# A spectral filter followed by a softmax-weighted linear layer: the order of the opening's loads, and where the filter's sums run

## The chip, the cores and the metric

The kernel runs on one core of a Trainium2 chip. The metric is the time of one execution in microseconds (us), the median of several runs. A core has TensorE (PE, matrix products; PEld is its weight load), VectorE (DVE), ScalarE (ACT), GpSimd (POOL) and SyncE (SP). Each works through its own queue of instructions in order. SP, ACT and POOL also issue DMA transfers; all of these run on the same 16 DMA engines of the core.

## The reference

```python
X = np.fft.rfft(x, axis=1)                    # x: (8, 3136, 256), float32
y = np.fft.irfft(X * (filt_r + 1j * filt_i)[None], n=3136, axis=1)
t = y.reshape(8 * 3136, 256)
h = t @ w_in                                  # w_in: (256, 1024), given in float64
e = np.exp(h - h.max(-1, keepdims=True))
solu = h * (e / (e.sum(-1, keepdims=True) + 1e-9))
ln = (solu - solu.mean(-1, keepdims=True)) / np.sqrt(solu.var(-1, keepdims=True) + 1e-6) * g_ln
out = ln @ w_out                              # w_out: (1024, 256), given in float64
```

Eight images of 3136 tokens with 256 channels are filtered in frequency space along the tokens; then each token goes through a layer of width 1024.

## The kernel before, in words

The transform of length 3136 is split into 49 x 64. For each image there are four steps, each a matrix product with a fixed table: a first one over 49 rows (`first`), stored to a DRAM buffer d1; a second one over 64 (`forward`), whose result is multiplied by the filter (`multiply`); the second one back (`inverse`), stored to a DRAM buffer d2; and the first one back (`back`), which writes the tokens into the tile `y`. The layer then runs over `y` in blocks of 128 tokens (`product`, `exponential`, `normalize`, `project`); while it works on one image, the four steps of the next images are fitted between its blocks by a written plan.

The change touches the **opening**: the four steps of image 0, for which there is no layer work to lie beside, and the preparation of tables and weights. The order on each engine is as written in the source (a manual schedule; waits come from the data).

- *x.* `fetch_x` (line 527) reads image 0 in eight pieces of four columns (L530). A piece has two halves of 49 rows in the tile `rows_x`: h = 0 in order, h = 1 in reversed order. Before, SP issues h = 0 (48 rows of each piece, and the 49th row of all pieces as one 32 KB transfer) and POOL issues h = 1. Between POOL's pieces stand the loads of two raw weight blocks (`begin`, L420).
- *Stage one.* For each piece two matmuls (L233), one copy by ACT from PSUM over the piece itself (L235), and a store to d1 in two parts: 96 rows by ACT (L188), 4 rows by SP (L189). PSUM has three buffers for this.
- *Tables and filters.* `load_tables` (L476, L479) reads one table and eight blocks of filter rows for four or five row groups: (0, 4) and (4, 4) by POOL, (8, 5) by SP.
- *Idle matmuls.* `idle_row(5)` and later `idle_row(14)` (L558) are matmuls whose result nobody reads; one more stands in front of each `inverse`.
- *The spectrum loop* (lines 586 to 609) has seven units. For each: a fetch of d1 (L298), `forward` on PE (L308, tile pb), `multiply` (four multiplications on DVE, L329 and L330; and two sums, L331, the first of which runs on DVE and the second on POOL), `inverse` (L308, tile pc), copies by ACT (L346) and the store to d2 (L350). In PE's queue `forward` of unit i + 2 stands ahead of `inverse` of unit i. The products use two buffers each. `tables_back` (L492) turns the tables for the way back, by a matmul with the unit matrix `one`.
- *Weights.* The weights come as float64 words, in eight blocks; `convert` (lines 425 to 456) makes float32 of one: seven or eight operations on DVE, for blocks 0 to 3 one on ACT (L451) and two on POOL (L452, L456), for blocks 4 to 6 one on POOL. Conversions 0 and 1 stand ahead of the loop, the others behind it, with `weight_sums` (L152).
- *Behind the loop.* SP fetches d2 (L358) once the stores of d2 have landed, then six pieces of the second image's x (L471); PE runs `back` (L404, tile py) behind the idle row; then the layer's first product (L754) and its first operation on DVE (L778).

[...]

Of the kernel before, what the change touches and what calls it, by code (L numbers as in the profile page):

```python
# [9 lines left out]
FP32 = mybir.dt.float32  # L10
# [7 lines left out]
P = 128  # L18
# [76 lines left out]
def kernel(  # L95
# [95 lines left out]
    class Spectrum:  # L191
# [24 lines left out]
        def fetch_x(self, i, halves, out=None):  # L216
            if out is None:
                out = self.pools["r"].tile([P, NCH, C], FP32, name=f"x_{self.e}_{i}", tag="r")
            self.xs[i] = out
            xb = x[self.e]  # L220
            for h, first, step in ((0, NCH * i, C), (1, N2 - 1 - NCH * i, -C)):
                halves[h](out[N1 * h:N1 * h + N1],
                          bass.AP(tensor=xb.tensor, offset=xb.offset + first * C,
                                  ap=[[N2 * C, N1], [step, NCH], [1, C]]))
# [186 lines left out]
    with ExitStack() as st:  # L411
# [53 lines left out]
        def spare_piece(i):  # L465
            return spare[i % 2][:, i // 2 * NCH * C:(i // 2 + 1) * NCH * C].rearrange(
                "p (n c) -> p n c", c=C)
# [6 lines left out]
        def load_tables(i0, n, dma):  # L474
            de = fpool.tile([P, n, 2, 2, NQ], FP32, name=f"de_{i0}", tag=f"de{i0}")
            dma(out=de[:, :, 0].rearrange("p i u q -> p i (u q)"), in_=there_dram[:, i0:i0 + n, :])  # L476
            f = fpool.tile([P, n, 2, C], FP32, name=f"f_{i0}", tag=f"f{i0}")
            for place, k, held, rows in all_filter_rows(i0, n):
                dma(out=f[place, 0:held, k, :], in_=rows)  # L479
            for i in range(n):  # L480
                tables[i0 + i], filters[i0 + i] = (de, i), (f, i)
# [36 lines left out]
        def begin(j):  # L518
            raws[j] = load_words(weights[j][1], j)
# [13 lines left out]

        st.enter_context(tc.manual_schedule())
        nc.sync.dma_start(out=wf_t, in_=wf_dram)
        nc.scalar.dma_start(out=one, in_=one_dram)
        pieces = NH // NCH

        fetch_x(0, 0, NCH, 0, N1 - 1, nc.sync.dma_start)
        fetch_x(0, 0, NH, N1 - 1, 1, nc.sync.dma_start)  # L540
        for i in range(pieces):
            if i:
                fetch_x(0, NCH * i, NCH, 0, N1 - 1, nc.sync.dma_start)
            fetch_x(1, NCH * i, NCH, 0, N1, nc.gpsimd.dma_start)
            if i in (4, 7):
                begin(i // 7)
        load_tables(0, 4, nc.gpsimd.dma_start)
        load_tables(4, 4, nc.gpsimd.dma_start)
        for i in range(pieces):
            sp.xs[i] = rows_x[:, NCH * i:NCH * i + NCH]  # L550

# [4 lines left out]
        def idle(out):  # L556

            nc.tensor.matmul(out=out, lhsT=tables[0][0][:, 0, 0].rearrange("p u q -> p (u q)"),  # L558
                             rhs=filters[0][0][:, 0], start=True, stop=True)

        def idle_row(count, name):
            for j in range(count):
                idle(ps_h.tile([P, 2, C], FP32, name=f"{name}_{j}", tag="h"))

        idle_row(5, "idle")

        def convert(j):
            load_float64(weights[j][0], raws.pop(j), negate=j < 4, share=j < 4,
                         add=(nc.vector if j == 7 else nc.gpsimd).tensor_tensor)

        for j in range(2):
            convert(j)

        def start(i):
            sp.fetch_filter(i)
# [3 lines left out]
        units = len(sp.units)  # L579

        sp.fetch(0, nc.sync.dma_start)
        for i in range(1, units - 2):
            sp.fetch(i, nc.sync.dma_start, spare_piece(i - 1))
            if i == 3:
                load_tables(8, NP - 8, nc.sync.dma_start)
        for i in range(2):
            start(i)
            tables_back(4 * i, 4)
        for i in range(units):
            if i == 2:  # L590
                tables_back(8, NP - 8)
            if i + 2 < units:
                start(i + 2)
            sp.multiply(i, 0, nc.vector.tensor_tensor)
            sp.multiply(i, 1, nc.gpsimd.tensor_tensor)
            pss = [ps_t.tile([P, 2, C], FP32, name=f"pc_0_{i}_{u}", tag="t") for u in range(2)]
            idle(pss[0])
            sp.inverse(i, pss)
            sp.store(i, nc.scalar.dma_start)
            if i == 0:  # L600
                nc.gpsimd.dma_start(out=wi_t, in_=wi_dram)
                nc.gpsimd.dma_start(out=wq_t, in_=wq_dram)
                nc.gpsimd.dma_start(out=wb_t[:, 0:N1], in_=wb_dram)
                nc.gpsimd.dma_start(out=g_sb, in_=moe_g_ln.rearrange("(k p) -> p k", p=P))
            elif i == 1:
                for last_one in (units - 2, units - 1):
                    sp.fetch(last_one, nc.gpsimd.dma_start, spare_piece(last_one - 1))
            for j in {2: (2,), 3: (3, 4), 4: (5,), 5: (6,)}.get(i, ()):
                begin(j)
        idle_row(14, "idler")  # L610
        rows_t4 = pools["r"].tile([P, NH, C], FP32, name="t4_0", tag="r")
# [5 lines left out]
        for i0, n, rows in ((0, 4, P), (4, 4, P), (8, NP - 9, P), (NP - 1, 1, NQ)):  # L617
# [2 lines left out]
                out=f_dram[i0:i0 + n].rearrange("i u q k c -> (u q) i (k c)")[0:rows],  # L620
                in_=f[0:rows, at:at + n].rearrange("p i k c -> p i (k c)"))
        convert(2)
        convert(3)
        begin(7)
        convert(4)
        weight_sums(w_in_sb)
        for j in (5, 6, 7):
            convert(j)
        for ch in range(pieces):
# [537 lines left out]
```

## Time and profile before

| what | value |
|---|---|
| median of 3 runs | 1595.84 us (1594.65 to 1599.87) |
| span of the profiled execution | 1598.0 us |
| its span against the median | 2.2 us longer; no time around the span is listed |
| PE busy | 1548.0 us, 97% |
| DVE busy | 1310.2 us, 82% |
| POOL busy | 1177.0 us, 74% |
| ACT busy | 915.8 us, 57% |
| DMA | 311.14 MB, mean 195 GB/s |
| first matmul on x | at 11.76 us |
| first product of the layer on PE | at 97.05 us |

How to read it: the span runs from the first to the last recorded instruction. "Busy" of an engine is the time in which it works; a wait is not busy. In a timeline row stand the start, the length, the engine, the source line, the operation and the tiles (result <- operands), and in brackets how long the engine had been idle and what ended it; "x16" means that neighbouring rows of one kind are merged. "SPq" is an issue by SP's queue. In a row of the windows view stand the stretch, its length, the busy time of PE, PEld, DVE, ACT and POOL with the number of instructions, the granted TensorE clock as a share of full speed, the mean busy share of the 16 DMA engines, and the GB/s that they moved. The landing of a transfer is the time of its last completion signal in the trace.

### The profile page before, as it was taken

The page shows a single profiled execution, that of the slowest core. Times are in us where ns is not written, and L with a number is a line of the kernel's source. Part 1 is how long each engine was busy: PE and PEld are TensorE (multiplying, and loading weights), DVE is VectorE, ACT ScalarE, POOL GpSimd, SP SyncE. Part 2 cuts the span into 40 slices and gives each one's busy share as a digit, 9 for nine tenths or more (in the row PEclk, how much of TensorE's full clock was granted, in tenths as well). Part 3 has the DMA queues.
Part 4 walks back from the last instruction along what each step waited for, and adds up shares of the span by engine and source line. Part 5 has one row for each costly group of instructions (what it writes and reads, how often), then busy time and mean ns, then how long its engine had stood idle before and what let it go on. Part 6 is the DMA issues. An engine that isn't in the chain of part 4 may idle for free. (4 is left out here: it accounts for less than half of the span.)

```text
span 1598.0 us, 37061 instructions
## 1 busy us (share of the span) xinstructions
PE 1548.0 (97%) x12828; PEld 1055.5 (66%) x12828; DVE 1310.2 (82%) x2639; ACT 915.8 (57%) x1825; POOL 1177.0 (74%) x1371
## 2 busy tenths in 40 slices
PE   5998999999999999999999999999999999999997
PEld 1463567666666676667766776667776777777777
DVE  1887888998998889888988889987898777777773
ACT  2245655656565656565566656665555666665653
POOL 4555986688768867886778877886866867677775
PEclk8999999999999999999999999999999999999999
DMA  9989978776987588766886678766784544343434
GB/s 261 288 272 261 262 214 236 215 228 175 247 245 231 157 230 238 230 177 169 235 240 195 166 196 256 209 183 174 222 220 127 134 125 127 96 113 99 113 103 115
DMA packets 343804, 311.14 MB, mean 195 GB/s; under 512 B 27835, under 2 KB 310100, under 8 KB 343620
## 3 DMA queue, kind: packets, MB, share of 16 engines
q1 hardware_dynamic: 271476, 170.45, 40.4%
q0 software_dynamic: 33744, 98.81, 20.6%
q10 hardware_dynamic: 38400, 39.53, 8.2%
q8 instruction: 104, 1.70, 0.5%
q14 instruction: 80, 0.65, 0.1%
HBM read 124.51 MB, written 81.40 MB: 129 GB/s over the span
## 5 line engine op out<-in xcount | busy, mean ns | idle before, releaser
L885 PEld LDWEIGHTS o<-w_out_sb,solu_t 128*128 128x128 f32 x3136 | 381.5, 192 | 50.2 <-issue 43.2
L885 PE MATMUL o<-w_out_sb,solu_t 128*128 128x128 f32 x3136 | 401.5, 276 | 3.8 <-DVE ot L905 3.1
L754 PE MATMUL m<-w_in_sb,s 128*128 128x512 f32 x784 | 397.9, 608 | 2.1 <-ACT h L764 1.4
L885 PEld LDWEIGHTS o<-w_out_sb,u 128*128 128x128 f32 x2352 | 305.9, 191 | 140.7 <-issue 104.0
L802 DVE SCALAR_TENSOR_TENSOR h<-e,rsum,h 128x1024 f32<-128x1024 f32 x196 | 321.2, 1639 | 6.9
L885 PE MATMUL o<-w_out_sb,u 128*128 128x128 f32 x2352 | 310.4, 275 | 3.0 <-POOL u L733 2.1
L754 PE MATMUL m<-w_in_sb,y 128*128 128x512 f32 x588 | 306.6, 604 | 3.0 <-DVE h L775 2.1
L764 ACT COPY h<-m 128x512 f32<-128x512 f32 x294 | 173.2, 589 | 201.8 <-PE m L754 193.6
L901 ACT ACTIVATE ot<-o,rs_t 128x128 f32<-128x128 f32 x392 | 143.2, 366 | 248.0 <-PE o L885 244.6
L733 POOL TENSOR_TENSOR u<-solu_t 128x512 f32<-128x512 f32 x98 | 133.5, 1362 | 178.3 <-DMA solu_t<-turn 157.0
L810 ACT ACTIVATE h<-h,nmu 128x1024 f32<-128x1024 f32 x196 | 224.6, 1146 | 47.0 <-DVE turn L818 37.4
L818 DVE STREAM_TRANSPOSE turn<-h 128x1024 f32<-128x1024 f32 x196 | 243.1, 1241 | 3.1
L778 DVE CUSTOM_DVE_ANT_0 h<-m,h 128x512 f32<-128x512 f32 x196 | 133.2, 679 | 131.6 <-ACT h L764 94.5
L786 ACT ACTIVATE e<-h,nmax 128x1024 f32<-128x1024 f32 x196 | 225.1, 1148 | 20.1 <-DVE h L802 18.8
L733 POOL TENSOR_TENSOR u<-solu_t,u 128x512 f32<-128x512 f32 x98 | 147.6, 1506 | 94.0 <-PE o L885 94.0
L754 PEld LDWEIGHTS m<-w_in_sb,s 128*128 128x128 f32 x784 | 127.9, 190 | 88.0 <-issue 68.3
L905 DVE SCALAR_TENSOR_TENSOR ot<-o,rs_t,ot 128x128 f32<-128x128 f32 x299 | 103.7, 347 | 73.8 <-ACT ot L901 55.6
L733 POOL TENSOR_TENSOR u<-u,solu_t 128x512 f32<-128x512 f32 x98 | 152.0, 1551 | 15.2 <-PE o L885 7.2
L733 POOL TENSOR_TENSOR solu_t<-solu_t,solu_t 128x512 f32<-128x512 f32 x98 | 161.8, 1651 | 0.9
L754 PEld LDWEIGHTS m<-w_in_sb,y 128*128 128x128 f32 x588 | 96.3, 190 | 98.1 <-issue 54.7
L733 POOL TENSOR_TENSOR s<-y 128x128 f32<-128x128 f32 x196 | 97.9, 500 | 0.5
L381 PEld LDWEIGHTS py<-wb_t,t 50*64 50x64 f32 x3584 | 57.6, 134 | 42.9 <-issue 22.5
(126 smaller groups left out, 2001.6 us busy)
## 6 DMA issues: line engine op xcount, KB each, us to landing
solu_t<-turn SPq DMA_DIRECT2D x780, 128.0 KB
out_dram<-ot SPq DMA_DIRECT2D x196, 128.0 KB
t<-d POOLq DMA_DIRECT2D x112, 200.0 KB, 6.8
d<-x POOLq DMA_DIRECT2D x100, 200.0 KB, 5.0
f<-f_dram POOLq DMA_DIRECT2D x39, 512.0 KB, 8.2
t<-d ACTq DMA_DIRECT2D x37, 512.0 KB
d<-g POOLq DMA_DIRECT2D x36, 512.0 KB, 4.9
x<-in_x_dram SPq DMA_DIRECT2D x112, 98.0 KB
```

The costliest lines, as they stand in the source:

```text
L381: nc.tensor.matmul(out=views[g][64 * h:64 * h + 64, cb, i, :], lhsT=t4[rows, i, c0:c0 + 64], rhs=wb_t[rows, 0:N1], start=True, stop=True)
L733: nc.gpsimd.tensor_tensor(out=out, in0=in0, in1=in1, op=op)
L754: nc.tensor.matmul(out=ms[j, bank], lhsT=lhsT, rhs=w_in_sb[:, w, :], start=m in (1, 2, 7), stop=True, skip_group_check=True)
L764: nc.scalar.copy(out=h_half(k, i), in_=ms[j, 0])
L778: nc.vector.tensor_tensor_reduce(out=h_half(k, i), in0=ms[j, bank], in1=h_half(*kept), scale=1.0, scalar=sofar, op0=ALU.add, op1=ALU.min, ...
L786: nc.scalar.activation(out=e, in_=hs[k], func=AFT.Exp, bias=nmaxs.pop(k)[:, 1:2], scale=-1.0, accum_out=esum)
L802: nc.vector.scalar_tensor_tensor(out=solu, in0=e, scalar=rsum, in1=solu, op0=ALU.mult, op1=ALU.mult, accum_out=nmu)
L810: nc.scalar.activation(out=solu, in_=solu, func=AFT.Square, bias=nmu, scale=-float(DFF), accum_out=variances[g][:, i:i + 1])
L818: nc.vector.transpose(out=turns[g][:, :, i, :], in_=solus[k].rearrange("p (f j) -> p f j", j=32))
L885: nc.tensor.matmul(out=pos[p, bank], lhsT=lhs[:, f, :], rhs=w[:, f, :], start=f == 0 and (m in (1, 2, 7) or alone), stop=True, skip_group_ ...
L901: nc.scalar.activation(out=out_half(p, *to)[0], in_=pos[p, 0], func=AFT.Copy, scale=rs)
L905: nc.vector.scalar_tensor_tensor(out=ot, in0=pos[p, bank], scalar=rs, in1=out_half(p, *kept)[0], op0=ALU.mult, op1=ALU.add)
```

## The change

x goes first: both halves of a piece are issued in turn, h = 0 by SP and h = 1 by ACT, 48 rows each, and both 49th rows behind the first piece; `one` follows on ACT. POOL's first work is a copy of one column that waits until the fourth piece of x has landed (`once_landed`); then it issues the tables (0, 4). DVE fills a part of `y`, and two matmuls on it stand at the head of PE's queue. The idle row ahead of the loop has 6 matmuls instead of 5, and the idle matmul in front of each `inverse` has half the columns.

SP's order becomes: fetches of d1 for units 0 and 1, tables (4, 4), fetches 2 and 3, tables (8, 5), fetches 4 to 6, and four small constants that POOL fetched before. POOL waits until fetch 0 has landed, and then issues raw weight blocks 0 and 1; blocks 2 to 5 follow in the loop, behind units 1, 2, 4 and 5, block 6 behind conversion 2 and block 7 behind conversion 3. Conversions 0 and 1 move into the loop, behind units 2 and 4. Both sums of `multiply` run on POOL. `weight_sums` moves ahead of conversion 4.

```diff
@@ -533,19 +533,29 @@
 
         st.enter_context(tc.manual_schedule())
         nc.sync.dma_start(out=wf_t, in_=wf_dram)
+        pieces = NH // NCH
+
+        for i in range(pieces):
+            for h, dma in ((0, nc.sync.dma_start), (1, nc.scalar.dma_start)):
+                fetch_x(h, NCH * i, NCH, 0, N1 - 1, dma)
+                if i == 0:
+                    row, at = N1 * h + N1 - 1, N2 * (N1 - 1) + NH * h
+                    dma(out=rows_x[row:row + 1, ::-1 if h else 1, :], in_=x[0, at:at + NH, :].rearrange(
+                        "(o n) c -> o n c", o=1))
         nc.scalar.dma_start(out=one, in_=one_dram)
-        pieces = NH // NCH
-
-        fetch_x(0, 0, NCH, 0, N1 - 1, nc.sync.dma_start)
-        fetch_x(0, 0, NH, N1 - 1, 1, nc.sync.dma_start)
-        for i in range(pieces):
-            if i:
-                fetch_x(0, NCH * i, NCH, 0, N1 - 1, nc.sync.dma_start)
-            fetch_x(1, NCH * i, NCH, 0, N1, nc.gpsimd.dma_start)
-            if i in (4, 7):
-                begin(i // 7)
+
+        seen = small.tile([P, 1], FP32, name="seen", tag="seen")
+
+        def once_landed(ap):
+            nc.gpsimd.tensor_copy(out=seen[0:ap.shape[0]], in_=ap)
+
+        once_landed(rows_x[0:NR, NCH * 3, 0:1])
         load_tables(0, 4, nc.gpsimd.dma_start)
-        load_tables(4, 4, nc.gpsimd.dma_start)
+        warm = y[:, 0, 0:512]
+        nc.vector.memset(warm, 1.0)
+        for n in range(2):
+            nc.tensor.matmul(out=ps_t.tile([P, 512], FP32, name=f"warm_{n}", tag="t"), lhsT=warm[:, 0:P],
+                             rhs=warm, start=True, stop=True)
         for i in range(pieces):
             sp.xs[i] = rows_x[:, NCH * i:NCH * i + NCH]
 
@@ -556,20 +566,17 @@
         def idle(out):
 
             nc.tensor.matmul(out=out, lhsT=tables[0][0][:, 0, 0].rearrange("p u q -> p (u q)"),
-                             rhs=filters[0][0][:, 0], start=True, stop=True)
+                             rhs=filters[0][0][:, 0, 0:len(out.shape) - 1], start=True, stop=True)
 
         def idle_row(count, name):
             for j in range(count):
                 idle(ps_h.tile([P, 2, C], FP32, name=f"{name}_{j}", tag="h"))
 
-        idle_row(5, "idle")
+        idle_row(6, "idle")
 
         def convert(j):
             load_float64(weights[j][0], raws.pop(j), negate=j < 4, share=j < 4,
                          add=(nc.vector if j == 7 else nc.gpsimd).tensor_tensor)
-
-        for j in range(2):
-            convert(j)
 
         def start(i):
             sp.fetch_filter(i)
@@ -579,10 +586,19 @@
         units = len(sp.units)
 
         sp.fetch(0, nc.sync.dma_start)
-        for i in range(1, units - 2):
+        sp.fetch(1, nc.sync.dma_start, spare_piece(0))
+        once_landed(sp.t2s[0][:, 0, 0:1])
+        for j in range(2):
+            begin(j)
+        load_tables(4, 4, nc.sync.dma_start)
+        for i in range(2, 4):
             sp.fetch(i, nc.sync.dma_start, spare_piece(i - 1))
-            if i == 3:
-                load_tables(8, NP - 8, nc.sync.dma_start)
+        load_tables(8, NP - 8, nc.sync.dma_start)
+        for i in range(4, units):
+            sp.fetch(i, nc.sync.dma_start, spare_piece(i - 1))
+        for held, source in ((wi_t, wi_dram), (wq_t, wq_dram), (wb_t[:, 0:N1], wb_dram),
+                         (g_sb, moe_g_ln.rearrange("(k p) -> p k", p=P))):
+            nc.sync.dma_start(out=held, in_=source)
         for i in range(2):
             start(i)
             tables_back(4 * i, 4)
@@ -591,21 +607,15 @@
                 tables_back(8, NP - 8)
             if i + 2 < units:
                 start(i + 2)
-            sp.multiply(i, 0, nc.vector.tensor_tensor)
+            sp.multiply(i, 0, nc.gpsimd.tensor_tensor)
             sp.multiply(i, 1, nc.gpsimd.tensor_tensor)
             pss = [ps_t.tile([P, 2, C], FP32, name=f"pc_0_{i}_{u}", tag="t") for u in range(2)]
-            idle(pss[0])
+            idle(pss[0][:, 0, :])
             sp.inverse(i, pss)
             sp.store(i, nc.scalar.dma_start)
-            if i == 0:
-                nc.gpsimd.dma_start(out=wi_t, in_=wi_dram)
-                nc.gpsimd.dma_start(out=wq_t, in_=wq_dram)
-                nc.gpsimd.dma_start(out=wb_t[:, 0:N1], in_=wb_dram)
-                nc.gpsimd.dma_start(out=g_sb, in_=moe_g_ln.rearrange("(k p) -> p k", p=P))
-            elif i == 1:
-                for last_one in (units - 2, units - 1):
-                    sp.fetch(last_one, nc.gpsimd.dma_start, spare_piece(last_one - 1))
-            for j in {2: (2,), 3: (3, 4), 4: (5,), 5: (6,)}.get(i, ()):
+            if i in (2, 4):
+                convert(i // 2 - 1)
+            for j in {1: (2,), 2: (3,), 4: (4,), 5: (5,)}.get(i, ()):
                 begin(j)
         idle_row(14, "idler")
         rows_t4 = pools["r"].tile([P, NH, C], FP32, name="t4_0", tag="r")
@@ -620,10 +630,11 @@
                 out=f_dram[i0:i0 + n].rearrange("i u q k c -> (u q) i (k c)")[0:rows],
                 in_=f[0:rows, at:at + n].rearrange("p i k c -> p i (k c)"))
         convert(2)
+        begin(6)
         convert(3)
         begin(7)
+        weight_sums(w_in_sb)
         convert(4)
-        weight_sums(w_in_sb)
         for j in (5, 6, 7):
             convert(j)
         for ch in range(pieces):
```

## The prediction

> **What bounds the kernel now.** I read the windows view first, in stretches of ten microseconds, then the timeline of the first 105 us, then the landings of single transfers in the trace. The windows say where the kernel can still change.
>
> ```profile
> 0.00:10.00 10.00, 0.00 (x0) 0.00 (x0) 0.06 (x1) 0.00 (x0) 6.28 (x12) 1.00 0.83 171
> 10.00:20.00 10.00, 8.24 (x14) 3.04 (x15) 0.00 (x0) 3.58 (x4) 2.66 (x4) 1.00 1.05 220
> 20.00:30.00 10.00, 8.27 (x20) 2.96 (x18) 5.77 (x13) 5.80 (x6) 3.71 (x7) 1.00 1.02 388
> 30.00:40.00 10.00, 3.64 (x4) 1.00 (x4) 2.04 (x4) 1.23 (x2) 7.01 (x12) 0.53 0.85 268
> 50.00:60.00 10.00, 9.34 (x110) 5.68 (x103) 8.49 (x13) 3.42 (x8) 7.95 (x11) 1.00 1.01 291
> 200.00:1500.00 1300.00, 1288.83 (x11317) 898.06 (x11317) 1110.86 (x2245) 782.24 (x1573) 989.37 (x1152) 1.00 0.68 189
> ```
>
> The columns after the length are PE, PEld, DVE, ACT, POOL, granted clock, DMA share, GB/s. The last row is the rest of the kernel: PE is busy 1288.83 of 1300 us. Nothing there is edited, so what the opening saves or loses passes to the end. The opening is DMA's: its share is 0.83 to 1.05 from the start, at only 171 and 220 GB/s while x is read, and 388 once stores of d1 join the reads.
>
> ```profile
> 11.76 16.52 PE L233 MATMUL pa<-x,wf_t 98*100 98x512 f32 x32 [11.76 <-DMA x<-in_x_dram]
> 36.30 7.19 PE L558 MATMUL idle<-f,de 128*128 128x512 f32 x10 [8.02 <-DMA f<-in_filt_r_dram]
> 37.28 0.40 SPq L298 DMA_DIRECT2D t<-d  x1
> 44.63 0.69 DVE L329 TENSOR_TENSOR pr<-pb,f 128x512 f32<-128x512 f32 x1 [12.52 <-PE pb L308]
> 50.93 0.69 DVE L329 TENSOR_TENSOR pr<-pb,f 128x512 f32<-128x512 f32 x1
> 52.25 1.38 DVE L331 TENSOR_TENSOR pr<-pr,pt 128x512 f32<-128x512 f32 x1
> 68.09 0.41 DVE L432 TENSOR_SCALAR raw<-raw 128x512 int32<-128x512 int32 x1
> 68.32 0.77 POOL L331 TENSOR_TENSOR pi<-pi,pt 64x256 f32<-64x256 f32 x1 [0.33 <-DVE pt L330]
> 70.66 12.28 PE L558 MATMUL idler<-f,de 128*128 128x512 f32 x28
> 82.78 14.43 PE L404 MATMUL py<-wi_t,t 100*128 100x98 f32 x128
> 103.34 0.69 DVE L456 TENSOR_TENSOR w_out_sb<-w_out_sb,raw 128x512 f32<-128x512 f32 x1
> 103.95 0.68 DVE L778 CUSTOM_DVE_ANT_0 h<-m,h 128x512 f32<-128x512 f32 x1
> ```
>
> Read them as stations. Matmuls on x start at 11.76. The first fetch of d1 goes out at 37.28, because the last store of d1, issued at 29.73, lands at 37.26 behind table traffic. The filter's product starts at 44.63 (unit 2 at 50.93); DVE leaves it at 68.09, POOL's last sum ends at 69.09. From 68.09 DVE is busy without a gap with conversions 2 to 7, to 103.95, where it takes the first product. PE's own line is 70.66, 82.78, 97.05.
>
> **Stage one.** Removed from ahead of d1's last store: both raw loads (1.05 MB) and the second table set (1.28 MB). Added ahead of the stores: nine x transfers on ACT's queue. [...] x to there is five pieces, 1.97 MB: at 220 GB/s 9.0 us, from the first packet at 2.3, plus 1.2 from last packet to landing (the 32 KB row: packet ends 7.19, landed 8.40) and 0.8, half of that row's 1.69 us on its one DMA engine: 13.3. Issue 0.37, table load 1.28, copy 1.01: 16.0. Three PSUM buffers hold pieces 0 to 2, so PE starts piece 3 there; five pieces at 1.72 (the pitch of copies before, 19.73 to 21.44) end at 24.6, the copy at 25.7, the store is issued at 26.0. By bytes: 1.6 MB of x and tables left at 16 plus 3.07 of d1 at 400 GB/s end at 27.7, and 1.2 to land. **T, the first fetch, is 28.9** against 37.28 (bounds 27 and 31: ACT freed at 11.7 or 14.5, and the byte sum at 350 GB/s).
>
> The two warming matmuls cost nothing: PE has no work there. They may save part of 3.4 us (four pieces' halves at 0.86 instead of 0.43), but ACT's copy, not PE, releases piece 3, so I count zero. POOL's copy that waits for x's fourth piece holds back the first tables to about 12; they need 1.28 MB, some 8 us, and are wanted by the idle row at 24.6: covered by 4 us.
>
> [...]
>
> **From T to unit 2.** The fetch of 512 KB lands 4.1 after issue (37.28 to 41.48): 33.0. Eight forward matmuls 1.11; DVE starts unit 0 at 34.2, 10.4 earlier. Then SP's order bites. Before, fetches 0 to 3 were issued back to back; now the table set for units 2 and 3 (nine transfers, 1.31 MB) stands between fetch 1 and fetch 2. PE's queue holds pb_2 ahead of the first inverse, and DVE's unit 2 needs the buffer that this inverse frees. [...] In bytes: two fetches, tables, one fetch, 2.9 MB at 370 GB/s plus 1.1 and 1.2 of ends is T+10.1; with both raw loads, which POOL now issues when fetch 0 has landed, in between (1.05 MB, 2.8 us) T+13. I take T+12, as the raw loads start some 3 us after POOL issues them: **40.9**, against 44.79. PE has then stood idle 5 us, and the clock falls, as after 28.3 (0.53 in the row 30 to 40, matmuls of the idle row at 1.06 instead of 0.43). So pb_2 2.0, idle 0.9, half of the inverse 1.0: **unit 2 starts at 44.8**, against 50.93. Of 10.4 gained 6.1 are left.
>
> **The product.** Removed from DVE: one sum per unit, five of 0.69 to 0.74, one of 1.38, a small one of 1.00. Added to POOL at 1.28 each (0.77 the small one), 8.5 us. Moved into DVE's row, behind units 2 and 4: conversions 0 and 1, which lay in dead time at 21.84 and 27.91. Alone a conversion takes 3.96 (21.84 to 25.80); beside POOL's sums up to 7.0 (72.46 to 79.49, two operations of 0.43 taking 1.5, one of 0.69 taking 1.66). I take 4.9, nearer to the first, since POOL's two sums cover only its first 2.6 us. DVE: four multiplications a unit, 2.44. Unit 2 to 47.2, conversion 52.1, unit 3 54.5, unit 4 57.0 (fetch 4 lands by T+23 = 52, behind nine more table transfers; it binds only if over 3 us late), conversion 61.9, unit 5 64.3, unit 6 at 1.6: **65.9 against 68.09, 2.2 earlier**. POOL: the second conversion's two operations stand ahead of unit 5's sums: 63.2, a raw load's issue 0.8, two sums 2.6, a load 0.8, two small sums 1.5: **68.9 against 69.09**. The last inverse comes about 0.9 earlier, since its idle matmul is halved.
>
> **To the end.** PE's line: 14 idle matmuls as before, so py and the first product come 0.9 earlier; it had slack (1.24 us on x of the second image at 103.1). DVE's line keeps its 35.9 us: first product 2.2 earlier. DMA's line: fetches of d2 start when its last store lands (75.74); 2.2 earlier, as fewer raw loads are queued there, but raw 6, issued at 67.17 before, now falls among the fetches: 0.52 MB at 283 GB/s is 1.9, leaving 0.3. Between 0.3 and 2.2 I take 1.5. The constants fetched by SP instead of POOL, and the shorter idle matmuls (0.43 each, DVE or POOL sets the pace), count zero; without that cover they are 3 us for six. Sum: 1598.0 - 1.5 = 1596.5. The profiled span is 2.2 over the median 1595.84, so I forecast **1594.3**.
>
> **Rivals.** *Data come in time.* T at 27, fetch 2 at T+10.1 = 37.1, PE warm: pb_2 1.1, idle 0.4, 0.8: unit 2 at 39.4. Conversions at 4.0 make 19.3 instead of 21.1: DVE leaves at 58.7, POOL at 61.7, 7.4 earlier, less 0.4 for raw 6: 7.0, median 1588.8. For it: reads in 1 KB packets ran at 350 GB/s (40 to 44 us), and x's reversed half now comes so. Against: SP's in-order queue.
> *The conversions collide with the sums (slower).* Both take 7.0: DVE leaves at 70.1. POOL's share of a conversion waits for DVE and stands ahead of the next unit's sums, 4.2 and one unit's 2.6 more: last sum at 75.7, 6.6 late, py with it; less PE's 1.2 slack 5.4, median 1601.2. It decides when the stretch of both exceeds the 2.2 that DVE gains. For it: the rows at 72.46. Against: the first conversions need no POOL until near their end.
> *x is no earlier.* ACT, held by its own x transfers, starts copying at 18, T is 32: 3.1 later than forecast, 1.6 over now, median 1597.4. The change then only trades waits.
>
> **Chances.** Forecast 0.47, x no earlier 0.12, data in time 0.27, collision 0.14. About 0.3% (4.8 us) is what a measurement of this kernel can tell from no change: faster 0.27, same 0.59, slower 0.14. The range reaches nearly to both outer cases: 1588 to 1601.5.
>
> **What would show it.** Right: first copy of ACT near 15, first fetch of d1 near 29, DVE's unit 0 near 34, then a DVE wait of some 5 us on pb_2, with the clock at half; DVE's third conversion near 66. Wrong: no wait there (data in time), or conversions of over 6 us and POOL's last sum past 72 (collision), or a fetch of d1 after 31. If the stations move as forecast and the end does not, the line from d2's fetches to the second image was mis-sized.

## The result, and the profile after

| kernel | median | range | runs |
|---|---|---|---|
| before, beside it | 1597.86 us | 1594.65 to 1600.28 | 4 |
| changed | 1639.35 us | 1637.67 to 1640.49 | 4 |

The ratio is **1.0266** (95% interval 1.0246 to 1.0287): 42 us slower. The forecast was 1594.3 us, with a range up to 1601.5. The profiled execution of the changed kernel has a span of 1638.1 us. Lines up to the edit keep their numbers; behind it L558 is now L568, L733 L744, L754 L765.

The windows of the changed kernel (columns as before):

```profile
50.00:60.00 10.00, 9.27 (x77) 5.26 (x78) 4.91 (x8) 2.15 (x4) 2.67 (x2) 0.69 0.96 221
60.00:70.00 10.00, 6.10 (x56) 3.23 (x54) 5.58 (x10) 2.48 (x5) 0.04 (x1) 0.83 0.68 200
70.00:80.00 10.00, 4.85 (x29) 2.54 (x32) 5.43 (x8) 1.07 (x2) 7.98 (x7) 0.67 0.31 105
80.00:90.00 10.00, 4.06 (x27) 1.92 (x22) 5.43 (x12) 1.74 (x3) 6.00 (x6) 0.50 0.44 149
200.00:1500.00 1300.00, 1278.97 (x11265) 885.43 (x11264) 1109.08 (x2221) 770.71 (x1553) 993.23 (x1153) 1.00 0.74 192
```

Two things are to be seen. From 60 to 90 us nothing is full: in one of the three rows POOL works 0.04 us of ten, in another the DMA share falls to 0.31, and PE and DVE are half idle throughout; so there is a chain of waits. And in the long last row, where no line was edited, PE is busy 1278.97 us instead of 1288.83, with a DMA share of 0.74 instead of 0.68 for nearly the same GB/s (192 and 189).

Matched instruction by instruction with the kernel before, PE's work is 25.3 us late at its first product (122.33 against 97.05), 26.4 at 250 us, and some 40 at the end. So some 25 us are lost in the opening and 14 to 15 more, bit by bit, in the body, which is everything behind the first product. That product in the kernel before:

```profile
97.05 1.93 PE L754 MATMUL m<-w_in_sb,y 128*128 128x512 f32 x4
```

The stations of the changed kernel, in the timeline:

```profile
7.36 7.06 PE L233 MATMUL pa<-x,wf_t 98*100 98x512 f32 x12 [2.13 <-DMA x<-in_x_dram]
15.84 1.01 ACT L235 COPY x<-pa 100x1024 f32<-100x1024 f32 x1
25.16 1.01 ACT L235 COPY x<-pa 100x1024 f32<-100x1024 f32 x1 [2.53 <-DMA d<-x]
32.45 0.40 SPq L298 DMA_DIRECT2D t<-d  x1
38.49 0.69 DVE L329 TENSOR_TENSOR pr<-pb,f 128x512 f32<-128x512 f32 x1 [37.06 <-PE pb L308]
55.02 0.69 DVE L329 TENSOR_TENSOR pr<-pb,f 128x512 f32<-128x512 f32 x1 [10.06 <-PE pc L308]
91.35 0.89 POOL L331 TENSOR_TENSOR pi<-pi,pt 64x256 f32<-64x256 f32 x1
94.71 13.51 PE L568 MATMUL idler<-f,de 128*128 128x512 f32 x28
108.06 14.43 PE L404 MATMUL py<-wi_t,t 100*128 100x98 f32 x128
122.33 1.93 PE L765 MATMUL m<-w_in_sb,y 128*128 128x512 f32 x4
```

DVE's unit 0 is 6.1 us earlier than before (38.49 against 44.63), unit 2 is 4.1 later, POOL's last sum 23.0 later. What lies between the last two of these is the loop; its chain of waits, in the timeline:

```profile
57.42 0.59 DVE L432 TENSOR_SCALAR raw<-raw 128x512 int32<-128x512 int32 x1
63.35 2.01 PE L308 MATMUL pb<-y,de 64*64 64x256 f32 x16 [3.00 <-DMA y<-d]
66.44 0.45 PE L308 MATMUL pc<-pr,de 64*64 64x256 f32 x2
67.66 1.07 ACT L346 COPY g<-pc 128x512 f32<-128x512 f32 x2 [6.74 <-PE pc L308]
69.23 0.65 ACT L451 ACTIVATE raw<-raw 128x512 f32<-128x512 int32 x1 [0.50 <-ACT g L346]
69.96 1.29 POOL L452 TENSOR_TENSOR raw<-raw,power 128x512 f32<-128x512 f32 x1 [10.82 <-ACT raw L451]
73.16 1.27 POOL L331 TENSOR_TENSOR pr<-pr,pt 128x512 f32<-128x512 f32 x1
74.48 1.13 PE L308 MATMUL pc<-pr,de 64*64 64x256 f32 x4 [5.38 <-POOL pr L331]
83.90 1.29 POOL L452 TENSOR_TENSOR raw<-raw,power 128x512 f32<-128x512 f32 x1 [5.82 <-ACT raw L451]
```

Read it from POOL's 10.82 backwards. POOL stands at its part of conversion 0 (L452), which needs ACT's part (L451). That needed only DVE's first operation, done at 58.0; but in ACT's queue it stands behind the copy of unit 2's inverse (L346). That inverse (pc, 66.44) stands in PE's queue behind `forward` of unit 4, which waited for fetch 4 until 63.35. And behind L452 in POOL's queue stand all sums of unit 3, whose operands DVE has had ready since 65. They start at 73.16, and PE's next inverse waits for them. At 83.90 conversion 1 does it once more.

### The profile page after: what moved, and what is told of

Its sections match the earlier page's. It is cut to its first block, busy times and chain, and to the rows that moved or that the text cites. A ratio compares the mean times of both kernels' runs of the same rounds, so it can differ in the third digit from the quotient of the medians.

```text
span 1638.1 us, 37078 instructions
## 1 busy us (share of the span) xinstructions
PE 1566.2 (96%) x12834; PEld 1063.4 (65%) x12834; DVE 1314.4 (80%) x2633; ACT 913.7 (56%) x1825; POOL 1180.4 (72%) x1357
## 5 line engine op out<-in xcount | busy, mean ns | idle before, releaser
L765 PE MATMUL m<-w_in_sb,s 128*128 128x512 f32 x784 | 397.9, 609 | 5.0 <-ACT h L775 3.3
L813 DVE SCALAR_TENSOR_TENSOR h<-e,rsum,h 128x1024 f32<-128x1024 f32 x196 | 311.4, 1589 | 6.9
L765 PE MATMUL m<-w_in_sb,y 128*128 128x512 f32 x588 | 308.0, 607 | 6.0 <-DVE nmax L789 3.7
L744 POOL TENSOR_TENSOR u<-solu_t 128x512 f32<-128x512 f32 x98 | 137.2, 1400 | 199.4 <-DMA solu_t<-turn 122.9
L744 POOL TENSOR_TENSOR u<-solu_t,u 128x512 f32<-128x512 f32 x98 | 146.4, 1494 | 82.3 <-PE o L896 82.1
L765 PEld LDWEIGHTS m<-w_in_sb,s 128*128 128x128 f32 x784 | 127.9, 190 | 91.0 <-issue 67.0
L744 POOL TENSOR_TENSOR solu_t<-solu_t,solu_t 128x512 f32<-128x512 f32 x98 | 168.7, 1722 | 0.9
L765 PEld LDWEIGHTS m<-w_in_sb,y 128*128 128x128 f32 x588 | 96.1, 191 | 102.9 <-issue 52.1
L744 POOL TENSOR_TENSOR u<-u,solu_t 128x512 f32<-128x512 f32 x98 | 151.2, 1543 | 14.8 <-PE o L896 6.7
L916 DVE SCALAR_TENSOR_TENSOR ot<-o,rs_t,ot 128x128 f32<-128x128 f32 x299 | 103.6, 347 | 72.3 <-ACT ot L912 49.0
L744 POOL TENSOR_TENSOR s<-y 128x128 f32<-128x128 f32 x196 | 99.6, 508 | 1.9 <-DMA y<-in_x_dram 1.5
L381 PEld LDWEIGHTS py<-wb_t,t 50*64 50x64 f32 x3584 | 57.6, 134 | 42.9 <-issue 21.7
```

The source lines that it names most:

```text
L381: nc.tensor.matmul(out=views[g][64 * h:64 * h + 64, cb, i, :], lhsT=t4[rows, i, c0:c0 + 64], rhs=wb_t[rows, 0:N1], start=True, stop=True)
L744: nc.gpsimd.tensor_tensor(out=out, in0=in0, in1=in1, op=op)
L765: nc.tensor.matmul(out=ms[j, bank], lhsT=lhsT, rhs=w_in_sb[:, w, :], start=m in (1, 2, 7), stop=True, skip_group_check=True)
L813: nc.vector.scalar_tensor_tensor(out=solu, in0=e, scalar=rsum, in1=solu, op0=ALU.mult, op1=ALU.mult, accum_out=nmu)
L916: nc.vector.scalar_tensor_tensor(out=ot, in0=pos[p, bank], scalar=rs, in1=out_half(p, *kept)[0], op0=ALU.mult, op1=ALU.add)
```

## The experiments

**Theory A** has two parts. (1) The chain above: a conversion between two units ties POOL's sums to ACT's queue, ACT's to PE's, and PE's to a fetch. (2) The tile `seen`, four bytes wide, which the guard (`once_landed`) writes: in the built program it takes 4 buffers of 32 bytes in a pool ahead of nearly all others, so `x`, `turn`, `solu_t`, `raw` and the rest, which started on multiples of 256 bytes, start 128 bytes past one. The traces hold no addresses; what the shift does is read from runs that change it alone. The trace shows packets that could belong to it: 512 bytes on SP's queue took 37.3 ns in the mean of 400 to 1500 us, and 32.9 before. **Rivals**: B, the body's loss follows from the opening's lateness; C, fetch 4 and the conversions' DVE time make the loop long, not the tie to ACT; Q and D on the order of transfers, S and P on the sums, below.

All ratios are to the kernel before, run beside each kernel. "d1", "d2": issue of the first fetch; "f2": landing of fetch 2; "u2": DVE starts unit 2; "p": PE starts the layer's first product, where the opening ends; all in us, each from one profiled execution.

| run | ratio (95%) | d1 | f2 | u2 | d2 | p |
|---|---|---|---|---|---|---|
| before | 1 | 37.3 | 44.8 | 50.9 | 75.7 | 97.1 |
| changed | 1.0266 (1.0246 to 1.0287) | 32.5 | 49.8 | 55.0 | 96.0 | 122.3 |
| e1: changed, seen 256 bytes | 1.0109 (1.0088 to 1.0130) | 31.8 | 47.7 | 52.8 | 93.6 | 117.8 |
| e16: changed, no tile seen | 1.0140 (1.0110 to 1.0170) | 30.8 | 46.5 | 51.1 | 91.1 | 115.4 |
| e2: before, shift 128 | 1.0094 (1.0058 to 1.0130) | 37.0 | 47.6 | 52.9 | 78.3 | 99.9 |
| e14: the same again | 1.0108 (1.0080 to 1.0137) | 37.5 | 46.5 | 51.7 | 77.8 | 98.9 |
| e12: before, shift 64 | 1.0171 (1.0140 to 1.0202) | 37.0 | 47.2 | 51.9 | 82.3 | 104.6 |
| e15: the same again | 1.0181 (1.0142 to 1.0220) | 35.9 | 47.4 | 52.1 | 82.7 | 104.5 |
| e3: changed, no ACT share | 1.0136 (1.0092 to 1.0180) | 33.7 | 50.7 | 55.1 | 87.2 | 115.1 |
| e4: e1 and e3 together | 1.0063 (1.0047 to 1.0079) | 32.1 | 48.0 | 53.2 | 83.3 | 111.0 |
| e7: e4, tables back on POOL | 1.0073 (1.0051 to 1.0096) | 35.0 | 41.9 | 48.8 | 83.5 | 107.7 |
| e8: e4, first sum on DVE | 1.0080 (1.0055 to 1.0105) | 31.5 | 48.1 | 52.7 | 84.7 | 112.8 |
| e9: e1, conversions ahead | 1.0038 (1.0015 to 1.0062) | 34.9 | 47.8 | 53.1 | 77.4 | 100.5 |
| e13: e9, tables back on POOL | 1.0020 (0.9998 to 1.0042) | 36.1 | 42.6 | 50.0 | 72.0 | 94.5 |
| e5: before, sums alone | 0.9995 (0.9979 to 1.0010) | 34.8 | 44.4 | 50.2 | 75.6 | 96.7 |
| e6: before, x alone | 0.9976 (0.9958 to 0.9994) | 36.5 | 42.9 | 47.9 | 72.3 | 94.3 |
| e10: before, x and sums | 0.9974 (0.9957 to 0.9992) | 35.6 | 42.0 | 49.7 | 73.1 | 95.5 |
| e11: e6, tables later | 0.9996 (0.9982 to 1.0010) | 33.2 | 39.6 | 50.0 | 79.4 | 102.0 |

### The address

**e1.** 

> The changed kernel with one thing different: the small tile that the two guards write (seen) has 8 buffers of 32 bytes instead of 4, so that all on-chip tiles allocated behind it lie 256 bytes further than in the kernel before, and on multiples of 256 bytes again, instead of 128 bytes further. Theory A (the 128-byte shift slows the SP queue's 512-byte packets, 34 ns before and 38 ns after, in the whole program, and this costs the 14 us that the changed kernel loses between 100 us and the end): 1625 us (1620 to 1629), 512-byte packets back at 32 to 34 ns. Rival B (the later loss comes from images whose transfers collide because the opening ended 25 us late; the address has no part): 1639, within 4 us. On the opening alone: both expect the raised wait of GpSimd at 59 to 70 us to stay, so the first fetch of d2 no earlier than 90 us.

```diff
-        seen = small.tile([P, 1], FP32, name="seen", tag="seen")
+        seen = small.tile([P, 1], FP32, name="seen", tag="seen", bufs=8)
```

**e16.** 

> The changed kernel with the guards writing into a column of y that is not used yet, so that there is no tile seen and every tile lies where it lay in the kernel before. Theory A (only the start off a multiple of 256 bytes matters): the same as with seen in 8 buffers, 1.011 (1.008 to 1.014), 512-byte packets at 33 to 34 ns. If any shift matters: between 1.011 and 1.027 or below 1.008.

```diff
-        seen = small.tile([P, 1], FP32, name="seen", tag="seen")
+        seen = y[:, 1, 600:601]
```

**e2.** 

> The kernel before with one thing added: a tile of 4 bytes per partition in the pool of small tiles (4 buffers of 32 bytes), written once by VectorE at the start; it moves all tiles allocated behind it by 128 bytes. Nothing else of the change is in it. Theory A (the shift alone slows packets): 1612 us (1607 to 1617), 512-byte packets at 36 to 38 ns instead of 32 to 34. Rival B (the later loss follows from the opening's lateness): 1598, within 3 us.

```diff
     nc.vector.memset(neg_half, -0.5)
+    seen = small.tile([P, 1], FP32, name="seen", tag="seen")
+    nc.vector.memset(seen, 0.0)
```

**e12** is e2 with `bufs=2`. 

> The kernel before with a small tile added as in the run with the 128-byte shift, but in 2 buffers, so that all tiles behind it lie 64 bytes further, on 64 past multiples of 256. If any start off a multiple of 256 bytes costs the same: 512-byte packets at 36 to 38 ns, time 1612 to 1619. If 64 bytes are enough alignment and only 128 is bad: 34 ns and 1598 to 1603.

**e14** and **e15** are e2 and e12 once more, beside each other. 

> The run with the 128-byte shift of the kernel before, once more with more rounds, beside the 64-byte one. If the size of the loss belongs to the offset: 1.009 (1.007 to 1.011). If any offset off 256 bytes costs the same and the two runs differed by chance: between 1.009 and 1.017, with the other run's interval overlapping.

> The run with the 64-byte shift of the kernel before, once more with more rounds, beside the 128-byte one. If the size of the loss belongs to the offset: 1.017 (1.014 to 1.020). If any offset off 256 bytes costs the same: the same as the 128-byte run, within 0.4%.

Rival B falls on both sides. e1 keeps a late opening and loses no more in the body: it is 20.8 us late at its first product and 16.9 at the end of its span. e2 has nearly the opening of the kernel before and loses all the same: 2.8 us late at its first product, 20.1 at the end. The line of SP's hardware queue on the page (packets, MB, share of the 16 engines' span), of the changed kernel and of e1:

```profile
q1 hardware_dynamic: 275266, 172.55, 43.5%
```

```profile
q1 hardware_dynamic: 275266, 172.55, 40.3%
```

The same packets and the same bytes; only their time differs. The engines' own work on the moved tiles isn't slower: between 400 and 1500 us the median of a matmul of the last product (275 ns), of ACT's exponential (1148) and of DVE's transposition (1245) is the same in the kernel before, the changed one, e2 and e15. The middle of the program in the windows view, of the kernel before, the changed one, e1, e2 and e15 in that order (third number: PE busy; last but one: DMA share):

```profile
120.00:1560.00 1440.00, 1422.53 (x12082) 976.89 (x12080) 1221.87 (x2470) 866.34 (x1735) 1093.43 (x1267) 1.00 0.69 190
```

```profile
120.00:1560.00 1440.00, 1411.27 (x11945) 961.10 (x11944) 1215.63 (x2448) 850.52 (x1705) 1088.08 (x1265) 1.00 0.74 192
```

```profile
120.00:1560.00 1440.00, 1425.05 (x12047) 974.12 (x12046) 1228.33 (x2482) 864.20 (x1730) 1098.67 (x1282) 1.00 0.69 194
```

```profile
120.00:1560.00 1440.00, 1415.43 (x11983) 967.42 (x11982) 1221.42 (x2444) 855.60 (x1716) 1081.79 (x1264) 1.00 0.73 189
```

```profile
120.00:1560.00 1440.00, 1401.83 (x11875) 955.51 (x11874) 1203.06 (x2419) 843.34 (x1694) 1072.66 (x1251) 0.99 0.73 189
```

PE's busy time and the DMA share go with the address, not with the opening: 0.69 where tiles start on multiples of 256 bytes, 0.72 (e14) to 0.74 where they do not. e16 has no shift at all and e1 one of 256; their intervals overlap, and their 512-byte packets took 33.0 and 32.8 ns. So a shift alone does not cost: of the three that were tried 256 bytes left the packets as they were, 64 and 128 slowed them. Mended, the changed kernel gains 1.3 to 1.6%, or 20 to 25 us, more than the 14 expected: the body no longer loses, and the opening's transfers are quicker too (fetch 2 lands 2 to 3 us earlier, the first product starts 4.5 to 7 earlier).

The two offsets differ little in packets: 512 bytes on SP's queue took 37.0 ns at 128 past (e14) and 37.3 at 64 past (e15), against 32.9 in the kernel before. In time 64 past is dearer, 1.7 to 1.8% against 0.9 to 1.1%, twice each. Some 5 us of that difference are there at the first product (p), where POOL's 4 KB packets took 294 to 297 ns at 64 past and 263 to 268 at 128 past (means from 32 to 56 us); why it is dearer stays open.

### The conversions

**e3.** 

> The changed kernel with one thing different: the two weight conversions that stand in the loop (0 and 1) do their scaled product on VectorE in one instruction instead of one on ScalarE and one on GpSimd; GpSimd keeps only the last addition. Theory A (GpSimd's instruction of conversion 0 waits 10.8 us for ScalarE's, which stands in ScalarE's queue behind the copy of unit 2, which waits for PE, whose queue is held by the late landing of fetch 4; all sums of units 3 to 6 stand behind it): the sums of unit 3 start at 64 to 66 us instead of 73.2, the first fetch of d2 at 82 to 86 instead of 96, time 1627 (1623 to 1632). Rival C (fetch 4 landing at 63.2 and the conversions' VectorE time themselves make the loop long): first fetch of d2 at 92 to 96, time 1636 to 1640.

```diff
-            load_float64(weights[j][0], raws.pop(j), negate=j < 4, share=j < 4,
+            load_float64(weights[j][0], raws.pop(j), negate=j < 4, share=j in (2, 3),
```

**e4.** 

> The changed kernel with both: seen in 8 buffers (tiles on multiples of 256 bytes again) and no part of conversions 0 and 1 on ScalarE. Theory A with both parts independent: 1639 less 14 less 12 = 1613 (1607 to 1619). Rival B and C: 1632 to 1640. If the two are one loss counted twice, no lower than the lower of the two single edits.

**e9** is e1 with the edit below: the raw loads and conversions 0 and 1 back ahead of the loop. 

> The changed kernel with seen in 8 buffers (tiles on multiples of 256 bytes again) and the move of conversions 0 and 1 undone: both stand ahead of the loop again, with ScalarE's and GpSimd's share, and their raw loads follow the first table set on GpSimd's queue. The first sum stays on GpSimd, x on two queues, tables for units 2 and 3 on SP between fetch 1 and fetch 2. Theory A (what is left in the run with both mends, 11 us at the last inverse, is 2 us of late fetch 2 and 9 us of two conversions standing between units): units 2, 3, 4, 5 at 3 to 4 us from each other unless fetch 4 is awaited once, first fetch of d2 at 74 to 78, time 1600 (1597 to 1605). Rival Q (SP's order alone, fetch 2 at 48 and fetch 4 at 59 us, sets the loop whatever VectorE does): first fetch of d2 at 80 to 83, time 1608 to 1612.

```diff
         load_tables(0, 4, nc.gpsimd.dma_start)
+        for j in range(2):
+            begin(j)
...
+        for j in range(2):
+            convert(j)
+
         def start(i):
...
-        once_landed(sp.t2s[0][:, 0, 0:1])
-        for j in range(2):
-            begin(j)
...
-            if i in (2, 4):
-                convert(i // 2 - 1)
```

In e3 the tie is gone, and with it one POOL operation of 1.29 us for each of the two conversions; DVE has one of 0.69 more instead. Its timeline:

```profile
62.60 0.69 DVE L454 SCALAR_TENSOR_TENSOR raw<-raw,power 128x512 f32<-128x512 int32 x1
63.36 1.29 POOL L456 TENSOR_TENSOR w_in_sb<-w_in_sb,raw 128x512 f32<-128x512 f32 x1 [4.14 <-DVE raw L454]
65.18 1.28 POOL L331 TENSOR_TENSOR pr<-pr,pt 128x512 f32<-128x512 f32 x1
```

POOL waits 4.14 us, for DVE, and unit 3's sums start at 65.18 instead of 73.16, as A said; by rival C they would have stayed late. The first fetch of d2 comes 8.7 us earlier (10.3 from e1 to e4), not quite the 10 to 14 expected, as the conversions still hold DVE between units. e4 came out at 1612.1 us where 1613 was expected, but beside a kernel before of 1602.6, not 1598. By the ratios both mends give 2.0%, 32 us of the 42. The ratio that is left is lower than after either mend alone, so they are two losses; but 2.0% is less than the sum of the single mends (1.6 and 1.3%), so they overlap in part. In e9 nothing stands between the units, and the first fetch of d2 comes 5.9 earlier still, the first product 10.5; so rival C keeps a part. The intervals of e4 and e9 overlap, so by time alone this step isn't shown; from e1 to e9, the whole move of the conversions, it is (1.0109 to 1.0038).

### The order on SP, and the sums

**e7** is e4 with the edit below. 

> The kernel of the run with both mends, with one more thing undone: the table set for units 2 and 3 is issued by GpSimd directly behind the first set, as in the kernel before, and no longer by SP between fetch 1 and fetch 2 of d1. Theory Q (SP's in-order queue is why fetch 2 lands 16 us after fetch 0 is issued, and this delays unit 2): fetch 2 lands at 40 to 43 us instead of 48, unit 2 at 45 to 48 instead of 53.2, first fetch of d2 at 77 to 80 instead of 83.3, time 1606 (1602 to 1609, with that run at 1612). Rival D (the DMA engines are full at 36 to 56 us whatever the order, share 0.8 to 1.08; the tables only move ahead of d1's stores and delay fetch 0 by what they save later): fetch 0 issued at 35 to 37, first fetch of d2 at 82 to 85, time 1610 to 1615.

```diff
         load_tables(0, 4, nc.gpsimd.dma_start)
+        load_tables(4, 4, nc.gpsimd.dma_start)
...
-        load_tables(4, 4, nc.sync.dma_start)
```

**e8** is e4 with the first sum on `nc.vector.tensor_tensor`. 

> The kernel of the run with both mends, with the first sum of the product back on VectorE. Theory S: VectorE is not gapless before 60 us here, so only units 3 to 6 count: 0.69 us each added, but GpSimd is freed of 1.26 each behind the conversions; first fetch of d2 within 2 us of 83.3, time 1610 to 1615. Rival P (GpSimd's serial sums behind its conversion additions are what is left of the loss): first fetch of d2 at 78 to 81, time 1605 to 1609.

**e13** is e9 with the tables back on POOL, behind the raw loads. 

> The run with the conversions ahead of the loop, with one more thing undone: the table set for units 2 and 3 is issued by GpSimd behind the first set and the raw loads, not by SP between fetch 1 and fetch 2. Theory Q (what that run still loses, 0.4%, is SP's order: fetch 2 landed at 47.8 us and fetch 4 at 59.7, so unit 2 starts at 53.1 and unit 4 waits until 62.6): unit 2 at 47 to 50, unit 4 at 56 to 60, first fetch of d2 at 72 to 75, time 0.997 to 1.001 of the kernel before. Rival R (the loss comes behind the opening, from constants on SP and the second image's first fetch, which that run waited 4.5 us for): first fetch of d2 earlier, but time still 1.002 to 1.006.

e7: fetch 2 landed 6 us earlier and unit 2 began 4.4 earlier, nearly as Q said, but all of it was lost again by the first fetch of d2, and there and in time it came out as rival D said, with the first fetch of d1 2.9 later. In the trace unit 4 waited 5.2 us for the inverse of unit 2, which stands behind `forward` of unit 4 in PE's queue; that could begin only at 59.5, when fetch 4 (59.3) and unit 3, held up by the conversion, were both through. With the conversions out of the way, e13 shows what SP's order cost. DVE's units 2, 3 and 4 in e9, then in e13:

```profile
53.09 0.69 DVE L329 TENSOR_TENSOR pr<-pb,f 128x512 f32<-128x512 f32 x1 [6.00 <-PE pc L308]
56.33 0.69 DVE L329 TENSOR_TENSOR pr<-pb,f 128x512 f32<-128x512 f32 x1 [0.75 <-PE pc L308]
62.61 0.69 DVE L329 TENSOR_TENSOR pr<-pb,f 128x512 f32<-128x512 f32 x1 [3.80 <-PE pc L308]
```

```profile
49.95 0.69 DVE L329 TENSOR_TENSOR pr<-pb,f 128x512 f32<-128x512 f32 x1 [1.40 <-PE pc L308]
52.53 0.69 DVE L329 TENSOR_TENSOR pr<-pb,f 128x512 f32<-128x512 f32 x1
57.35 0.69 DVE L329 TENSOR_TENSOR pr<-pb,f 128x512 f32<-128x512 f32 x1 [2.35 <-PE pc L308]
```

The waits of 6.00 and 3.80 are those for fetches 2 and 4 (47.8 and 59.7 in e9; 42.6 and 52.4 in e13). The first fetch of d2 is 5.4 us earlier than in e9, and 3.7 earlier than in the kernel before; yet e13 is not faster than the kernel before. PE's work in it, 2.6 us ahead at the first product, is some 1 us behind at 250. In e9 a fetch of the second image was awaited 4.5 us at 140. What eats the gain behind the opening (rival R) was not taken apart. e8's time does not tell it from e4, but its first fetch of d2 (84.7) is no earlier: S said so, and by P, the sums in series on POOL as what is left of the loss, it would have come at 78 to 81.

### Parts alone

**e5** is the kernel before with the first sum on `nc.gpsimd.tensor_tensor`. 

> The kernel before with one part of the change alone: the first sum of the filter's product goes to GpSimd, as the second did already. Theory S (VectorE sets the pace of the loop from 59.4 us, so each sum taken from it there, 0.69 us for units 3 to 6, is gained as long as GpSimd's two sums of 1.26 stay under VectorE's 2.7 per unit): first fetch of d2 2 us earlier than 75.7, time 1596 (1593 to 1598 when the kernel before is at 1598). Rival P (the sums in series on GpSimd lengthen the path from product to inverse by 0.6 us per unit and by GpSimd's raw loads): first fetch of d2 0 to 3 us later, time 1598 to 1601.

**e6** is the kernel before with the changed kernel's loop over x, and behind it: 

> The kernel before with one part of the change alone: x comes by the SP and ScalarE queues in the order of the changed kernel; raw loads 0 and 1 and both first table sets follow on GpSimd's queue, in their old order, behind a guard on the fourth piece of x (its tile has 8 buffers, so addresses stay on multiples of 256 bytes). Everything behind is as before: conversions 0 and 1 ahead of the loop, first sums on VectorE. Theory X (x on two queues makes d1 complete some 4 us earlier, and the gain reaches the loop because nothing is moved into SP's queue): first fetch of d1 at 33 to 35 instead of 37.3, first fetch of d2 2 to 4 us earlier, time 1595 (1592 to 1597 when the kernel before is at 1598). Rival Y (the bytes of the raw loads and tables, now behind x, fall on d1's stores): first fetch of d1 at 36 to 39, time 1597 to 1601.

```diff
+        seen = small.tile([P, 1], FP32, name="seen", tag="seen", bufs=8)
+        nc.gpsimd.tensor_copy(out=seen[0:NR], in_=rows_x[0:NR, NCH * 3, 0:1])
+        for j in range(2):
+            begin(j)
         load_tables(0, 4, nc.gpsimd.dma_start)
         load_tables(4, 4, nc.gpsimd.dma_start)
```

**e10** is e5 and e6 together. 

> The kernel before with two parts of the change together: x by the SP and ScalarE queues with the guard in 8 buffers (as in the run with x alone), and the first sum on GpSimd (as in the run with the sums alone). Conversions, tables of units 2 and 3, constants and the order of fetches as before. If the parts only add: 1598.1 less 1.3, so 0.997 of the kernel before (0.995 to 0.999). If GpSimd, which now also carries the raw loads behind x, becomes the bound of the loop: 0.999 to 1.003.

**e11** is e6 with the edit below. 

> The run with x alone (kernel before, x by the SP and ScalarE queues), with one more thing: the table set for units 2 and 3 is issued by GpSimd only when fetch 0 of d1 has landed, not behind the first set. Theory Y (1.28 MB of tables fall on d1's stores, at some 300 GB/s 4 us): first fetch of d1 at 32 to 34 instead of 36.5, unit 2 at 44 to 47 instead of 47.9, time 0.995 to 0.998 of the kernel before. Rival D (the bytes only move from ahead of fetch 0 to behind it, and fetches 2 and 3 then wait for them): unit 2 at 47 to 50, time 0.998 to 1.002.

```diff
-        load_tables(4, 4, nc.gpsimd.dma_start)
...
         sp.fetch(0, nc.sync.dma_start)
+        nc.gpsimd.tensor_copy(out=seen, in_=sp.t2s[0][:, 0, 0:1])
+        load_tables(4, 4, nc.gpsimd.dma_start)
```

The sums alone change nothing in the time that can be measured; DVE leaves the loop 1.1 us earlier (67.0 against 68.1), but the first fetch of d2 stays at 75.6, where S had it 2 us earlier. x alone gains 0.24%: the first fetch of d1 hardly moves (36.5: the raw loads and tables now fall on d1's stores, as rival Y said), but fetch 2 lands 1.9 earlier and the first fetch of d2 comes 3.5 earlier. e11 shows both halves of that trade: fetch 0 goes out 3.3 earlier and unit 2 starts 2.2 later, as rival D said. In e10 the two parts add up (0.9974). **e6 and e10 are faster than both kernels**, by a quarter of a per cent, with intervals that end at 0.9994 and 0.9992.

## Why the prediction was wrong

- *"Nothing there is edited, so what the opening saves or loses passes to the end."* **This step failed**: the body lost 14 to 15 us more. The price of the address in the whole time is 1.3 to 1.6% by e1 and e16, 0.7% once the tie to ACT is gone (e3 to e4). The diff edits no line of the body, but a tile of four bytes moves the others, and packets of 512 bytes take 37.3 ns instead of 32.9. I priced the guard's wait and not its tile.
- *The product, POOL's line* ("the second conversion's two operations stand ahead of unit 5's sums: 63.2"). **Failed:** POOL's last sum ended at 92.24 instead of 68.9. I let POOL wait for DVE alone. ACT's part was given no place in ACT's queue, and so no tie to PE and fetch 4. Worth 8.7 to 10.3 us at the first fetch of d2; in time 1.3% (e3), or 0.5% once the address is mended (e1 to e4). The rival "collide" had the place right, POOL's part ahead of the next sums, and one of its two signs came, POOL's last sum past 72; but it had the wrong cause: the conversions took 5.2 and 5.6 us, near the 4.9 forecast, not 7.0. Its 7.0 was read from a stretch (72.46 to 79.49) in which POOL did not run the filter's sums but its own parts of conversions, L452 and L456.
- *Fetch 2 at T+12.* Mis-sized: T+17.3. SP issued it at T+7.2, and it then took 10.1 us to land, where the sum of the bytes had it landed by T+13 at the latest. Fetch 4 *"binds only if over 3 us late"*, by T+23 = 52: it landed at 63.2, T+30.8, and bound. Of T+17.3, 1.4 belong to the address (T+15.9 in e1 and e4).
- *T = 28.9.* 32.45, outside the bounds of 27 to 31. ACT's first copy ended at 16.85 instead of 16.0. That it comes behind five pieces of x was an estimate, which no run tests by itself; in the changed kernel the fifth reversed piece, issued at 7.13, landed at 13.99, and ACT issued `one` at 14.01. The pitch was 1.46 instead of 1.72; but ACT's fifth store of d1 waited for its first one to land (24.68, issue at 24.75; ACT's copy behind it is the row with 2.53), which I had not put into the sum, and the last store was issued at 29.10 instead of 26.0. That T fell near the 32 of the rival "x is no earlier" is chance: there ACT was to start copying at 18, and it started at 15.84.
- *Unit 0 at 34.2, unit 2 at 44.8*: 38.49 and 55.02, for the most part by the two terms above. Besides, unit 0's `forward` took 2.0 us instead of 1.11, behind a PE idle for 4.0 us (granted clock 0.50 from 36 to 39), and unit 2 started 5.3 us after fetch 2 instead of 3.9.
- *The sums.* The price was right (1.25 to 1.27 each, one of 1.44, against 1.28), and so was their small effect (e5). The warm matmuls, the constants and the shorter idle matmuls were not tried alone.
- *PE's line to the end.* The idle row took 13.51 us instead of 12.28, as the clock was at half when it began (0.50 in the row 80 to 90, and still from 94.71 to 97); 1.2 us more that I had at nothing.
- *Two small slips.* The fetch from 37.28 to 41.48 takes 4.2 us, not 4.1, and the 0.4 for raw 6 in the rival "data come in time" has no working, where the forecast has 1.9 for the same load.

Of the 42 us, the address and the tie to ACT's queue together take 32. Which of the two is larger, the times do not tell (e1 and e3 overlap). In the profiled executions the body's 14 to 15 us go with the address: with it mended the body loses nothing (e1) to 1.6 us (e4, e16). The 25.3 at the first product fall by 4.5 with the address mended (e1), by 6.8 more without the tie (e4), by 10.5 with the conversions ahead of the loop (e9), and by 6.1 with the tables back on POOL (e13), 2.6 past the kernel before. (The idle row took 14.72 us in e4 and 12.28 in e1 and e9; without these 2.4 us the second step would be 9.2 and the third 8.1.) So the rest in time (0.6% in e4) is the conversions' place, SP's order and what follows behind the opening, in shares that the times do not separate.

## What to carry to other kernels

Before pricing a change, compare where the tiles lie in both programs: here a new tile of four bytes alone made the kernel before 0.9 to 1.1% slower (e2, e14), with packets of 512 bytes at 37.0 ns and more instead of 32.9. When work is moved between the turns of a loop, write down for each engine that takes part which instruction stands ahead of it in that queue, and follow the waits until they end at a transfer; the length of the moved work is only a part of its price (here its place cost 5.9 us and its tie 10.3, at the first fetch of d2). A gain at the head of a chain (unit 0 here 6 us earlier) is worth nothing until the next thing that ends last has been found.

## What was not expected of the hardware

Starting 128 or 64 bytes past a multiple of 256, packets of 512 bytes on SP's queue took 37.0 to 37.6 ns instead of 32.6 to 33.1, packets of 1 KB 54 to 55 instead of 52 to 53, and those of 4 KB on POOL's queue 218 to 223 instead of 213 to 218 (means from 400 to 1500 us over all runs). In the kernel before this cost 0.9 to 1.1% of the whole time at 128 and 1.7 to 1.8% at 64, in a kernel whose PE is busy 97%: with PE's waits for its operands in the trace, between 120 and 1560 us, at 16.5 us before, 27.6 in the changed kernel and 13.9 in e1.
